# A spectral filter and token MLP with its backward pass on one core: half of the column tables by symmetry, the first turned tile in quarters, four row moves issued by GpSimd, eleven fillers moved forward

## The chip, the core and the metric

The kernel runs on one core of a Trainium2 chip. The core has TensorE (PE; its weight loads are listed as PEld), VectorE (DVE), ScalarE (ACT), GpSimd (POOL) and SyncE (SP), which run their own instruction streams in order and wait for each other by semaphores; DMA transfers are issued by one of them and carried out by 16 DMA engines. The metric is device time in microseconds (us) of one execution; lower is better. The time before is the median of three runs, 345.46 us (343.97 to 347.54).

## The reference

Forward and gradient of two residual blocks on x of 2048 x 448 in bf16 (S = 2048 tokens, D = 448, F = 1792):

```
h  = x + irfft2( rfft2( layernorm(x) ) * (w_r + i w_i) )        # over both axes, 225 columns kept
h2 = h + ( gelu( layernorm(h)^T w1 + b1 ) w2 + b2 )^T            # the MLP mixes tokens
out, vjp = jax.vjp(f, x, w_r, w_i, w1, b1, w2, b2)
return out, *vjp(grad_out)
```

Eight outputs: h2 and the gradients of x, w_r, w_i, w1, b1, w2 and b2. The two-dimensional transform is done as matmuls with tables of sines and cosines.

## The kernel before

**Stages.** The forward transform has a *row part* and a *stage 2*. In the row part the 16 row tiles of x (128 rows of 448) are normalized, folded (left half plus and minus the mirrored right half, `fold_prep`; from the fifth pair on in quarters, `fold_quarters`), and go through two steps on TensorE: `row_a(t)` multiplies the fold by a 128 x 128 table scaled by the row's standard deviation (`scale_R`), and `row_b(h)` multiplies by the column tables `csF` (or `csQ`, the even columns of them, reordered by GpSimd at line 926). csF has sine and cosine (index w, cosine 0, sine 1), two blocks b, and KW = 226 columns, and is made by `gen_fwd_d`: VectorE computes the angles and reduces them, ScalarE takes the Sin. Each pair of row_b steps fills one tile `cs`, which a DMA moves into `D2` with its rows spread over 32 partitions (line 689, eight moves of 226 KB; the tiles lie in the buffers r452, rX). Stage 2 (`s2_stage`) is a transform over the other factor of the rows: for five steps s, 48 small matmuls out of D2, ScalarE copies, VectorE multiplies with the filter W, 48 small matmuls back, and moves into `D3` (line 727, sixteen of 113 KB, issued by GpSimd). Then `inv_rows` transforms D3 back, and the MLP and the backward pass follow, from 96 us on.

**Fillers.** Independent of all this is the first product of the backward MLP, grad_out times w2 transposed: 14 column tiles j of w2 with 16 matmuls of 448 columns each, 224 in all. `dg_gen` is a generator which gives one of them at each step, and `fill(n)` puts n of them into TensorE's stream at that place. FILL_A and FILL_B say how many stand ahead of and behind each row step t; more stand between the tables and in stage 2 (7 and 7 in each of its five steps), and `drain()` behind stage 2 puts out what is left, 37 of them behind the last 7 of stage 2. w2 must be transposed for it: tiles 0 to 3 come as they are and are turned on TensorE (`turn_w2`, 16 transposes of 128 x 128 in two groups of eight, each copied from PSUM by ScalarE at line 319), tiles 4 to 13 by a transposing DMA (line 312) into a ring of five buffers (three in rE, two in rO): tile j + 5 is loaded when tile j is used up, but no more than CAP tiles before the rows are done; the ones held back are loaded in front of the last 14 fillers ahead of stage 2.

**Order.** The streams of TensorE, VectorE, ScalarE and SP keep the order in which the program calls them; GpSimd's is set by a planner. A move into D2 is put off by RESH_LAG = 1.1 us of TensorE's planned time (`defer`) and then stands in SP's stream. So that stream has in one line the transposing DMAs, the 18 loads of W (line 591) and the D2 moves. `evac` gives a PSUM copy to ScalarE or VectorE by a running sum of estimated costs, so a change ahead of it can turn over who copies what.

Names that matter below: `D2` lies in r2 (matmuls from it are listed at line 225, `ps_ff<-r,Vt`), `D3` in r3 (`ps_ff<-RTm,r` at line 220 is its first use), fillers are `ps_mm<-rC,rE` or `rC,rO` at line 220, row_a is `ps_ff<-rX,rS`, row_b `ps_ff<-csF,rS` or `ps_ff<-r,rS`. VectorE's and ScalarE's operations nearly all have line 84, a recording helper.

Of the kernel before, what the change touches and what calls it, by code (L numbers as in the profile page):

```python
# [12 lines left out]
I32 = mybir.dt.int32  # L13
# [8 lines left out]
KW = 226  # L22
# [4 lines left out]
KC = 113  # L27
# [10 lines left out]
CAP = 9  # L38
# [86 lines left out]
def kernel(  # L125
# [188 lines left out]
    def turn_w2(j, parts=(0, 8)):  # L314
        for h in parts:
            pt = (ps_mm if j < 2 else ps_ff)()[:].bitcast(BF16).rearrange("p (t c) -> p t c", c=P)
            for t in range(8):
                nc.tensor.transpose(pt[:, t, :], w2n[j][:, h + t, :], ident[:])
            sc.copy(out=w2Ts[j][:, h:h + 8, :], in_=pt)
# [54 lines left out]
    for _ in range(20):  # L374
# [6 lines left out]
             channel_multiplier=0, allow_small_or_imprecise_dtypes=True)  # L381
    krow = ftmp(0, D)
# [49 lines left out]

    def gen_fwd_d(late):
        t = ftmp(576, 2, KW)
        t2 = ftmp(1028, 2, KW)
        q = ftmp(1536, 2, KW)
        q2 = ftmp(2048, 2, KW)
        js = []
        for o in (1.0, 225.0):
            js.append(col())  # L440
            ve.tensor_scalar(out=js[-1], in0=pcol, scalar1=2.0 / 896.0, scalar2=o / 896.0, op0=ALU.mult, op1=ALU.add)
        chains = []
        s_ = Later(sc, late)
        for w, u, v, ph in ((1, t, q, 0.0), (0, t2, q2, 0.25)):
            chain = []
            v_ = Later(ve, chain)
            for b in range(2):
                v_.tensor_scalar(out=u[:, b, :], in0=krow[:, 0:KW], scalar1=js[b], scalar2=ph, op0=ALU.mult, op1=ALU.add)
            v_.tensor_scalar(out=v, in0=u, scalar1=MAGIC, scalar2=MAGIC, op0=ALU.add, op1=ALU.subtract)
            v_.tensor_tensor(out=v, in0=u, in1=v, op=ALU.subtract)  # L450
            s_.activation(out=csF[:, w, :, :], in_=v, func=ACT.Sin, scale=s1)
            chains.append(chain)
        for pair in zip(*chains):
            for fn in pair:
                fn()
        s_.copy(out=csF[:, 0, :, 0:1], in_=rAT[:, 0:2].rearrange("p (b o) -> p b o", o=1))
# [209 lines left out]
    def row_b(h, quarters=None):  # L666
# [21 lines left out]
        if c:  # L688
            defer(RESH_LAG, lambda: resh[0].dma_start(out=D2[u:u + 125:4, 8 * e:8 * e + 8].rearrange("p g c k -> p (g c k)"),
                                                      in_=cs.rearrange("p x c k -> p (x c k)")), cs)  # L690
# [133 lines left out]
    def dg_gen():  # L824
        pgs = {}
        turns = {(0, 3): 1, (1, 11): 2, (2, 4): 3}
        order = [(j, 4 * q + i) for q in range(4) for j in range(2) for i in range(4)]
        for j, t in order + [(j, t) for j in range(2, NFB) for t in range(NT)]:
            if not t:
                pgs[j] = ps_mm()  # L830
            mm(pgs[j][:, 0:D], lhsT=w2Ts[j][:, t, :], rhs=go_tp[:, t, :], start=(t == 0), stop=(t == NT - 1))
            if (j, t) in turns:
                turn_w2(turns[j, t])
            if t == NT - 1:
                evac(out=dgu[:, j, :], in_=pgs.pop(j)[:, 0:D])
                if w2T_ring.i >= cap[0]:
                    held_w2.append(load_w2T)
                else:
                    load_w2T()
            yield  # L840
# [10 lines left out]
    for fn in r_ops:  # L851
        fn()
    ve.tensor_scalar(out=ident[:], in0=krow[:, 0:P], scalar1=pcol, scalar2=None, op0=ALU.is_equal)
# [17 lines left out]
    turn_w2(0, (0,))  # L871
# [4 lines left out]
    turn_w2(0, (8,))  # L876
# [26 lines left out]
    FILL_B = (0, 0, 0, 2, 2, 2, 2, 2, 2, 2, 2, 2, 2, 2, 2, 2)  # L903
# [531 lines left out]
```

## Time and profile before

| | us |
|---|---|
| median of 3 runs | 345.46 (343.97 to 347.54) |
| profiled execution | 345.03 |
| its span (first to last instruction) | 343.3 |
| TensorE busy in the span | 329.5 |
| VectorE / ScalarE / GpSimd busy | 250.8 / 206.7 / 73.7 |

By stage, from the view of busy time in windows (us from the start of the span; DMA is the mean busy share of the 16 DMA engines, by packet times that can overlap):

| stage | window | TensorE busy | VectorE busy | ScalarE busy | DMA |
|---|---|---|---|---|---|
| loads, first rows | 0 to 16.2 | 12.8 | 14.4 | 12.1 | 0.91 |
| rows 4 to 9 | 16.2 to 31.7 | 14.1 | 15.1 | 11.4 | 1.00 |
| rows 10 to 15 | 31.7 to 43.5 | 11.8 | 7.1 | 8.3 | 1.03 |
| tables, until stage 2 | 43.5 to 50.3 | 4.6 | 3.0 | 3.1 | 1.04 |
| stage 2 | 50.3 to 70.8 | 20.2 | 15.0 | 14.9 | 1.12 |
| fillers behind it | 70.8 to 79.1 | 8.3 | 1.3 | 3.5 | 0.54 |
| inverse rows | 79.1 to 96.0 | 16.3 | 13.1 | 15.5 | 0.98 |
| MLP and backward pass | 96.0 to 343.3 | 241.3 | 181.8 | 137.9 | 0.88 |

The granted TensorE clock was 1.00 in every window. In a line of a stream the first two numbers are start and duration in us, then engine, line, operation, output and inputs, and how many are merged; in square brackets stands the idle time of the engine before it and what ended it. A line with SPq or POOLq is the issuing of a DMA, not its transfer.

### The profile page before, as it was taken

The page shows a single profiled execution, that of the slowest core. Times are in us where ns is not written, and L with a number is a line of the kernel's source. Part 1 is how long each engine was busy: PE and PEld are TensorE (multiplying, and loading weights), DVE is VectorE, ACT ScalarE, POOL GpSimd, SP SyncE. Part 2 cuts the span into 40 slices and gives each one's busy share as a digit, 9 for nine tenths or more (in the row PEclk, how much of TensorE's full clock was granted, in tenths as well). Part 3 has the DMA queues.
Part 4 walks back from the last instruction along what each step waited for, and adds up shares of the span by engine and source line. Part 5 has one row for each costly group of instructions (what it writes and reads, how often), then busy time and mean ns, then how long its engine had stood idle before and what let it go on. Part 6 is the DMA issues. An engine that isn't in the chain of part 4 may idle for free.

```text
span 343.3 us, 7935 instructions
## 1 busy us (share of the span) xinstructions
PE 329.5 (96%) x2868; PEld 173.6 (51%) x2877; DVE 250.8 (73%) x669; ACT 206.7 (60%) x447; POOL 73.7 (21%) x235
## 2 busy tenths in 40 slices
PE   8798979999999999999999999999999999999995
PEld 4475644456645555555555555554333334555552
DVE  8999438724966888594325988786589985599993
ACT  5987647856966553513221346565488875688882
POOL 7766202441220000001001111110000000156660
PEclk9999999999999999999999999999999999999999
DMA  7999999979899999767976988836898898999975
GB/s 265 397 171 179 173 262 174 185 144 253 242 346 307 333 278 253 177 204 221 207 179 137 169 190 180 169 96 186 223 288 236 214 262 244 295 238 295 231 289 203
DMA packets 138606, 78.03 MB, mean 227 GB/s; under 512 B 88072, under 2 KB 130440, under 8 KB 138440
## 3 DMA queue, kind: packets, MB, share of 16 engines
q1 hardware_dynamic: 137000, 75.28, 86.9%
q0 software_dynamic: 1280, 1.86, 3.0%
q8 instruction: 22, 0.36, 0.5%
q10 hardware_dynamic: 288, 0.39, 0.3%
q14 instruction: 16, 0.13, 0.1%
HBM read 27.81 MB, written 22.04 MB: 145 GB/s over the span
## 4 chain that ended last, share of the span: by engine, by line
PE 69%; DVE 2%; ACT 1%; issue 1%; POOL 0%; DVEq 0%; ACTq 0%
PE ps_mm L220 62%; PE ps_ff L220 6%; PE ps_ff L225 2%; DVE rA L84 1%; ACT rO L84 1%; DVE r L84 0%; ACT rC L84 0%; DVE rS L84 0%; DVE rO L84 0%; DVE rB L84 0%; POOL lcol L1183 0%; ACT rAT L84 0%; DVEq L1430 0%; ACT r L84 0%; ACT rstd_h L84 0%
## 5 line engine op out<-in xcount | busy, mean ns | idle before, releaser
L220 PEld LDWEIGHTS <-r 128*128 128x128 bf16 (+2 forms) x628 | 58.5, 105 | 47.3 <-issue 2.8
L220 PEld LDWEIGHTS <-rS 128*128 128x128 bf16 (+1 forms) x468 | 36.2, 97 | 34.9 <-issue 6.4
L84 ACT CAST rO<-ps_mm 128x512 bf16<-128x512 f32 (+1 forms) x70 | 37.3, 583 | 15.9 <-PE ps_mm L220 14.1
L220 PE MATMUL ps_mm<-rD,r 128*128 128x448 bf16 x224 | 44.5, 352 | 0.0
L220 PEld LDWEIGHTS <-rst 128*128 128x128 bf16 (+1 forms) x320 | 23.5, 97 | 31.4 <-issue 14.1
L220 PE MATMUL ps_mm<-rC,rE 128*128 128x448 bf16 x144 | 31.5, 353 | 0.9 <-ACT rE L84 0.9
L220 PE MATMUL ps_mm<-rB,r 128*128 128x448 bf16 x160 | 31.2, 352 | 0.1
L220 PE MATMUL ps_mm<-rG,rst 128*128 128x512 bf16 (+1 forms) x121 | 26.8, 380 | 1.1 <-issue 0.8
L220 PE MATMUL ps_mm<-r,rst 128*128 128x512 bf16 (+2 forms) x144 | 27.4, 345 | 0.0
L84 ACT CAST r<-ps_ff 128x452 bf16<-128x452 f32 x44 | 23.9, 586 | 5.2 <-PE ps_ff L225 3.0
L84 ACT ACTIVATE r<-ps_mm,rstd_h 128x448 bf16<-128x448 f32 x16 | 10.1, 634 | 26.8 <-PE ps_mm L220 26.8
L84 DVE SCALAR_TENSOR_TENSOR r<-ps_mm,b2col,r 128x448 bf16<-128x448 f32 x16 | 10.9, 682 | 19.9 <-PE ps_mm L220 18.2
L84 ACT ACTIVATE r<-rC 128x448 bf16<-128x448 bf16 x16 | 9.1, 571 | 26.7 <-DMA out_dram<-r 22.5
L1183 POOL TENSOR_SCALAR lcol<-lcol 128x1 f32<-128x1 f32 x16 | 8.5, 530 | 64.7 <-ACT r L84 64.7
L84 ACT ACTIVATE rG<-rG 128x896 bf16<-128x896 bf16 x14 | 13.3, 950 | 14.9 <-DVE rG L84 14.7
L220 PEld LDWEIGHTS <-rO 128*128 128x128 bf16 (+1 forms) x165 | 15.2, 98 | 12.0 <-ACT rO L84 0.2
L220 PE MATMUL ps_ff<-csI,rAT 113*128 113x224 bf16 (+1 forms) x108 | 19.0, 298 | 0.6 <-ACT rAT L84 0.4
L84 ACT CAST rS<-ps_ff 128x512 bf16<-128x512 f32 x31 | 18.0, 584 | 2.0 <-PE ps_ff L220 1.7
L1356 POOL TENSOR_SCALAR lcol<-lcol 128x1 f32<-128x1 f32 x16 | 3.7, 234 | 70.7 <-ACT r L84 69.6
L220 PE MATMUL ps_mm<-rC,rO 128*128 128x448 bf16 x80 | 18.5, 353 | 0.0
L220 PEld LDWEIGHTS <-rE 128*128 128x128 bf16 x144 | 13.0, 98 | 10.6 <-ACT rE L84 1.2
L84 DVE TENSOR_SCALAR rG<-rG 128x896 bf16<-128x896 bf16 x28 | 10.9, 389 | 10.0 <-ACT rG L84 10.0
(197 smaller groups left out, 639.6 us busy)
## 6 DMA issues: line engine op xcount, KB each, us to landing
out_dram<-rO SPq DMA_DIRECT2D x34, 256.0 KB
r<-in_B_w_dram SPq DMA_DIRECT2D x5, 1024.0 KB
r<-r SPq DMA_DIRECT2D x12, 226.0 KB
r<-in_B_w_dram SPq DMA_DIRECT2D x3, 896.0 KB
rS<-in_B_w_dram SPq DMA_DIRECT2D x3, 896.0 KB
out_dram<-rG SPq DMA_DIRECT2D x10, 256.0 KB
rB<-in_B_w_dram SPq DMA_DIRECT2D x4, 512.0 KB
rO<-in_B_w_dram SPq DMA_DIRECT2D x2, 1024.0 KB
```

The source lines that it names most:

```text
L84: fn(**kw)
L220: nc.tensor.matmul(out, lhsT=lhsT, rhs=rhs, start=start, stop=stop)
L225: nc.tensor.matmul(out, lhsT=lhsT, rhs=rhs, start=start, stop=stop)
L1183: gp_.tensor_scalar(out=m1, in0=ms, scalar1=-1.0 / D, scalar2=None, op0=ALU.mult)
L1356: gp_.tensor_scalar(out=m1, in0=ms, scalar1=-2.0 / D, scalar2=None, op0=ALU.mult)
```

## The change

- `gen_fwd_d` computes 113 of the columns of each table (KC = 113) in one array instead of 226 in two, with one Sin for all; the other 112 are the mirrored columns of the other table (sine from cosine and the reverse), times +1 or -1 by the parity of the partition, in two VectorE copies. The column at the end is set to zero. The signs come from a GpSimd iota and two VectorE steps of one column.
- `turn_w2` takes groups of any size, and the first half of tile 0 is turned and copied in two groups of four. The first fillers are put in another order: tile 0 quarters 0 and 1, tile 1 quarters 0 and 1, then the others in turn.
- The four D2 moves with u >= 2 (the later half) are issued by GpSimd instead of SP.
- FILL_B gets 4 more fillers at row step 2, 3 at step 6, 2 each at steps 7 and 8; so `drain()` has 11 fewer. CAP is 10 instead of 9, which lets a tenth tile of w2 be loaded within the rows.

In the order of the instructions of the changed kernel, the load of that tenth tile stands in SP's stream between the third and the fourth D2 move, with loads of W around it, and the only GpSimd instruction between its four moves is a memset of csF's first column, which waits for the table's transposes (line 563 before). The two mirror copies stand in VectorE's stream behind the fold for rows 4 and 5. In the balance of copies, VectorE takes over three copies of row_a results and one of an inverse table, and gives up three row_b copies and one filler copy to ScalarE.

```diff
-CAP = 9
+CAP = 10
...
-    def turn_w2(j, parts=(0, 8)):
-        for h in parts:
+    def turn_w2(j, parts=((0, 8), (8, 8))):
+        for h, n in parts:
             pt = (ps_mm if j < 2 else ps_ff)()[:].bitcast(BF16).rearrange("p (t c) -> p t c", c=P)
-            for t in range(8):
+            for t in range(n):
                 nc.tensor.transpose(pt[:, t, :], w2n[j][:, h + t, :], ident[:])
-            sc.copy(out=w2Ts[j][:, h:h + 8, :], in_=pt)
+            sc.copy(out=w2Ts[j][:, h:h + n, :], in_=pt[:, 0:n, :])
...
+    podd = col().bitcast(I32)
+    gp_.iota(podd, pattern=[[0, 1]], base=0, channel_multiplier=1, allow_small_or_imprecise_dtypes=True)
+    gp_.memset(csF[:, :, :, KW - 1:KW], 0.0)
...
     def gen_fwd_d(late):
-        t = ftmp(576, 2, KW)
-        t2 = ftmp(1028, 2, KW)
-        q = ftmp(1536, 2, KW)
-        q2 = ftmp(2048, 2, KW)
+        u = ftmp(576, 2, 2, KC)
+        q = ftmp(1028, 2, 2, KC)
...
+        for w, ph in ((1, 0.0), (0, 0.25)):
             for b in range(2):
-                v_.tensor_scalar(out=u[:, b, :], in0=krow[:, 0:KW], scalar1=js[b], scalar2=ph, op0=ALU.mult, op1=ALU.add)
-            v_.tensor_scalar(out=v, in0=u, scalar1=MAGIC, scalar2=MAGIC, op0=ALU.add, op1=ALU.subtract)
-            v_.tensor_tensor(out=v, in0=u, in1=v, op=ALU.subtract)
-            s_.activation(out=csF[:, w, :, :], in_=v, func=ACT.Sin, scale=s1)
...
+                ve.tensor_scalar(out=u[:, w, b, :], in0=krow[:, 0:KC], scalar1=js[b], scalar2=ph, op0=ALU.mult, op1=ALU.add)
+        ve.tensor_scalar(out=q, in0=u, scalar1=MAGIC, scalar2=MAGIC, op0=ALU.add, op1=ALU.subtract)
+        ve.tensor_tensor(out=q, in0=u, in1=q, op=ALU.subtract)
+        Later(sc, late).activation(out=csF[:, :, :, 0:KC], in_=q, func=ACT.Sin, scale=s1)
+        v_ = Later(ve, late)
+        for w in range(2):
+            v_.tensor_scalar(out=csF[:, w, :, KC:2 * DC + 1], in0=csF[:, 1 - w, :, DC - 1::-1], scalar1=sgn, scalar2=None, op0=ALU.mult)
...
-            defer(RESH_LAG, lambda: resh[0].dma_start(out=D2[u:u + 125:4, 8 * e:8 * e + 8].rearrange("p g c k -> p (g c k)"),
+            defer(RESH_LAG, lambda: (gp_ if u >= 2 and quarters is csQ else nc.sync).dma_start(out=D2[u:u + 125:4, 8 * e:8 * e + 8].rearrange("p g c k -> p (g c k)"),
...
-        order = [(j, 4 * q + i) for q in range(4) for j in range(2) for i in range(4)]
+        order = [(j, 4 * q + i) for j, q in ((0, 0), (0, 1), (1, 0), (1, 1), (0, 2), (1, 2), (0, 3), (1, 3)) for i in range(4)]
...
+    ve.tensor_scalar(out=podd, in0=podd, scalar1=1, scalar2=None, op0=ALU.bitwise_and)
+    ve.tensor_scalar(out=sgn, in0=podd, scalar1=-2.0, scalar2=1.0, op0=ALU.mult, op1=ALU.add)
...
-    turn_w2(0, (0,))
+    turn_w2(0, ((0, 4), (4, 4)))
...
-    turn_w2(0, (8,))
+    turn_w2(0, ((8, 8),))
...
-    FILL_B = (0, 0, 0, 2, 2, 2, 2, 2, 2, 2, 2, 2, 2, 2, 2, 2)
+    FILL_B = (0, 0, 4, 2, 2, 2, 5, 4, 4, 2, 2, 2, 2, 2, 2, 2)
```

More of the change, by code (lines that the diff above doesn't have):

```diff
@@ L430, in gp_madd @@
         gp_.tensor_tensor(out=out, in0=gtmp, in1=in1, op=ALU.add)
+    sgn = col()
     def gen_fwd_d(late):
-        t = ftmp(576, 2, KW)
-        t2 = ftmp(1028, 2, KW)
-        q = ftmp(1536, 2, KW)
-        q2 = ftmp(2048, 2, KW)
+        u = ftmp(576, 2, 2, KC)
+        q = ftmp(1028, 2, 2, KC)
         js = []
@@ L441, in gen_fwd_d @@
             ve.tensor_scalar(out=js[-1], in0=pcol, scalar1=2.0 / 896.0, scalar2=o / 896.0, op0=ALU.mult, op1=ALU.add)
[L442 to L446, printed above, removed]
-            for b in range(2):
-                v_.tensor_scalar(out=u[:, b, :], in0=krow[:, 0:KW], scalar1=js[b], scalar2=ph, op0=ALU.mult, op1=ALU.add)
-            v_.tensor_scalar(out=v, in0=u, scalar1=MAGIC, scalar2=MAGIC, op0=ALU.add, op1=ALU.subtract)
-            v_.tensor_tensor(out=v, in0=u, in1=v, op=ALU.subtract)
-            s_.activation(out=csF[:, w, :, :], in_=v, func=ACT.Sin, scale=s1)
[L452 to L456, printed above, removed]
+        for w, ph in ((1, 0.0), (0, 0.25)):
+            for b in range(2):
+                ve.tensor_scalar(out=u[:, w, b, :], in0=krow[:, 0:KC], scalar1=js[b], scalar2=ph, op0=ALU.mult, op1=ALU.add)
[5 more added lines that the diff above has]
+            v_.tensor_scalar(out=csF[:, w, :, KC:2 * DC + 1], in0=csF[:, 1 - w, :, DC - 1::-1], scalar1=sgn, scalar2=None, op0=ALU.mult)
+        Later(sc, late).copy(out=csF[:, 0, :, 0:1], in_=rAT[:, 0:2].rearrange("p (b o) -> p b o", o=1))
     def gen_R(ve, sc):
```

## The prediction

> **What bounds the kernel now.** I read the page's busy row first, then who TensorE waited for, then the streams of TensorE, SP and POOL one by one in order of time.
>
> ```profile
> PE 329.5 (96%) x2868; PEld 173.6 (51%) x2877; DVE 250.8 (73%) x669; ACT 206.7 (60%) x447; POOL 73.7 (21%) x235
> ```
>
> TensorE is busy for 329.5 of 343.3 us, so all idle time is 13.8 us, and the change neither adds nor removes a matmul of the fillers. It can only win idle time back. The waits of TensorE in the first 110 us (what, line, for whom: us in total, times, longest) say where that is:
>
> ```profile
> PE ps_ff L225 <- DMA r<-rX: 2.2, 1, 2.2
> PE ps_ff L220 <- ACT csF L84: 1.3, 1, 1.3
> ...
> PE ps_ff L220 <- DVE rS L84: 1.0, 2, 0.7
> PE ps_mm L220 <- ACT rE L84: 0.9, 2, 0.5
> ...
> PE ps_ff L220 <- DVE rX L84: 0.3, 1, 0.3
> ```
>
> 3.5 us lie in the row steps (1.3 + 1.0 + 0.9 + 0.3), all before 31.7 us; after that the rows run without a gap. Then comes 2.2 us before stage 2, for the last moves into D2. TensorE's stream in order of time (start, us) shows both ends of stage 2:
>
> ```profile
> 45.31 2.81 PE L220 MATMUL ps_mm<-rC,rE 128*128 128x448 bf16 x14
> 50.34 0.63 PE L225 MATMUL ps_ff<-r,Vt 32*32 32x452 bf16 x16 [2.22 <-DMA r<-rX]
> ...
> 70.79 5.47 PE L220 MATMUL ps_mm<-rC,rE 128*128 128x448 bf16 x28
> 76.09 3.19 PE L220 MATMUL ps_mm<-rC,rO 128*128 128x448 bf16 x16
> 79.12 0.83 PE L220 MATMUL ps_ff<-RTm,r 128*113 128x128 bf16 x12
> ```
>
> The rows end at 43.5; fillers last until 48.1; D2 is complete at 50.3. Behind stage 2, 44 fillers (28 + 16) cover the moves into D3 until 79.1. SP's stream shows why D2 is late, and when D3 has landed:
>
> ```profile
> 38.43 3.84 SPq L312 DMA_TRANSPOSE rO<-in_B_w_dram  x1
> 42.37 0.59 SPq L689 DMA_DIRECT2D r<-r  x1
> 43.01 1.91 SPq L591 DMA_DIRECT2D rW<-in_A_w_i_dram  x3
> 45.02 0.58 SPq L689 DMA_DIRECT2D r<-r  x1
> 45.65 0.60 SPq L591 DMA_DIRECT2D rW<-in_A_w_i_dram  x1
> 46.36 2.57 SPq L689 DMA_DIRECT2D r<-rX  x4
> 49.02 2.02 SPq L312 DMA_TRANSPOSE rO<-in_B_w_dram  x1
> ...
> 77.34 0.42 SPq L1016 DMA_DIRECT2D r<-in_B_w_dram  x1
> ```
>
> SP issues without a pause from 13.5 to 49.0; the four late moves wait in that line (their data were evacuated by 44.4), and the last, issued at 48.4, is there 1.9 us later. The load at 77.34 waits for all D3 moves, so D3 is complete at about 77.3: the cover behind stage 2 is 79.1 - 77.3 = 1.8 us longer than needed. For POOL's moves there is a row of its own (below: its stream, and the landing times of its 16 moves of 113 KB):
>
> ```profile
> 71.67 2.36 POOL L727 DMA_DIRECT2D r<-r  x4 [1.27 <-ACT r L84]
> ...
> DMA to landing us min/median/max: 3.7/5.8/7.5
> ```
>
> **Column tables.** VectorE's stream has four 128x226 steps (1.08 us from start to end), two of 128x452 (0.69) and two subtractions (1.16): 2.68 us from 7.91 to 10.59. After it are four of 128x113 (0.8, between 0.6 by the 128x1 row of 144 ns and 1.1 by the 128x226 row), one of 128x452 (0.35) and one subtraction (0.58): 1.7, so 0.95 saved (0.65 to 1.15). Added are two 128x1 steps ahead of ident (0.15 each; VectorE waited 0.26 for x there, so 0.1 counts) and, behind the second pair's fold, two mirror copies of 128x224 (0.25 each, between the 128x128 bf16 step's 0.22 and the 128x512 one's 0.31). These wait for ScalarE's Sin, now one of 452 where two took 1.03; it ends at about 15.5, VectorE comes at 15.6, so the wait is nothing (0 to 0.5). Queued behind the mirrors are the statistics and row scales of all later rows. Net: the fold for row 4 comes 0.85 earlier, everything behind it 0.35 earlier (0.9 earlier to 0.3 later). POOL's added iota and memset (0.14 and 0.1 by the rows beside them) lie ahead of krow, which VectorE uses a microsecond later: nothing.
>
> **First turned tile in quarters, and the new order of the first fillers.** ScalarE's copy of 1024 columns took 1.01 us and held TensorE 0.43; two of 512 cost some 0.55 each, and four fillers then need only the first half. The second wait of 0.45 goes too, since fillers 5 to 8 now use the other quarter of tile 0. I take 0.8 off (0.4 if the second quarter of grad_out is late).
>
> **Eleven fillers.** One costs 0.195 us (16 in 3.19, 28 in 5.47), so 2.15 us move from the cover behind stage 2 into rows that had 3.5 us idle. Four fill the gap before row 4, three that before row 8, two each those before rows 9 and 10. VectorE's chain sets those rows, so the rows end where they did: 43.4 (42.2 if every gap closes; 45.7 if none does and the fillers simply add).
>
> **D2, which decides.** SP loses four issues (2.57 us), but they were the last ones. With the cap at 10, a fifth transpose is issued between the last two moves that stay on SP. The one that was issued at 45.02 now stands behind it. A transpose took SP 2.0 to 3.8 us in this stretch, so that move goes out at 47.1 to 48.9, and lands 1.9 (the row before) to 3 us later: 49.0 to 51.9, middle 50.4. On POOL the last late move goes out when its evacuation ends, 44.4, plus one issue of 0.59 ahead of it: 45.0. Landing takes 3.7 to 7.5 for half the bytes, plus 0.4 for the other half (0.3 at the 386 GB/s that the moves reached at 49 us, 0.75 at the 150 GB/s of 71 to 76): 49.0 to 53.3, 51.2 at the median row; if POOL were as quick as SP with the same move (1.9), 46.9; the memset between the last two waits for the table's transposes at 43.7, which are past. D2 needs both, so I take the later middle, 51.2 against 50.3: **stage 2 starts 0.9 us later**, with 3 us idle before it. The DMA engines were 1.06 busy from 44.0 to 50.3. The Trainium skill's entry page, "Trainium Kernel Development and Optimization", Key Constraints, says that the queues of SP and GpSimd share the same 16 engines and that issuing from several saves only issue time; by it the move to POOL is worth at most SP's 2.57 us of issuing. POOL's rows show 3.7 to 7.5 us to landing for 113 KB; "DMA: Bandwidth & Descriptors" (Anatomy of one DMA) fits 2.0 us plus bytes/436e3 for a GpSimd DMA, which makes 2.5 us for 226 KB, an estimate that the rows contradict. By the page POOL's moves would be in by 47.5 and SP alone would decide.
>
> **Behind stage 2.** The cover shrinks by 2.15, of which 1.8 was spare; TensorE then waits 0.35 for D3. The first copy of the next stage, held up by a filler's evacuation (0.44 wait at 80.40), gains 0.2. The rest of the kernel, from 96 us on, is TensorE's and unchanged. The transposes that were behind the late moves come earlier, so no filler waits.
>
> **Sum**, against the profiled execution's 345.03 us (span 343.3): -1.8 (fillers off the tail) -0.2 (the copy) +0.9 (D2) = -1.1, giving 343.9. What VectorE and the quarters save is not added: it becomes wait for D2. The median of the runs, 345.46, is 0.43 above the profiled one, so the prediction is **344.4**.
>
> **Rivals.**
> 1. *D2 comes early.* If the moved issues free both queues, with the transpose at 2.0 us and POOL at its shortest rows, D2 is complete at 49.0, or 1.3 earlier than before: -2.0 - 1.3 = -3.3, 342.2. At best TensorE sets the start: rows end at 42.2 with all gaps closed, 4.6 of fillers and table transposes behind them make 46.8, and -5.5, 340.0. For it: POOL's last four moves in the trace, with no other traffic, took 4.2. Against: here a transpose is under way.
> 2. *POOL's moves land late (slower).* Place: the last move, with a transpose on the same engines. At 7.5 us plus 0.8 and the 45.0 issue it is 53.3; with the two moves ahead of it still under way another 1.2 (two times the 0.59 issue pace): 54.5. Stage 2 starts 4.2 later, -2.0 + 4.2 = +2.2: 347.7. It decides from D2 at 52.3 on, where the gain of 2.0 is used up.
> 3. *The rows don't take the fillers.* If the folds are no earlier and the fillers fall beside the gaps, rows end at 45.7, POOL issues 2.2 later, D2 is complete at 53.4 and the gain is gone: -2.0 + 3.1 = +1.1, 346.6.
>
> **How the numbers follow.** Forecast (D2 between 50.2 and 52.2) 0.50, 343.4 to 345.4; rival 1 0.25; rival 2 0.15; rival 3 0.10. The range 341.8 to 346.9 leaves out the better half of rival 1 and the worse half of rival 2. 1% (3.45 us) is about what a measurement of this kernel can tell from no change. Faster than 342.0 needs D2 below 48.8, the better half of rival 1, with POOL near SP's 1.9: 0.15. Slower than 348.9 needs D2 beyond 55.8, the end of rival 2: 0.08. The rest, 0.77, lies between.
>
> **What would show it.** In the profile after: waits of TensorE on csF, rS, rX and rE down from 3.5 to about 1 us; the wait before stage 2 at 2 to 4 us, released by a move from POOL or the last one on SP; that one issued near 48 behind a transpose; POOL's moves with landings of 4 to 8 us; a short new wait of the RTm matmuls for D3. The prediction is wrong if the wait before stage 2 is under 1 us, or if POOL's landings pass 9 us.

## The result: 1.1% slower, and the profile after

The changed kernel takes 349.74 us (median of 4 runs, 347.72 to 352.09) where the kernel before takes 345.19 (4 runs): a ratio of 1.0112, 95% interval [1.0063, 1.0160]. The forecast was 344.4, the range ended at 346.9. The profiled execution took 348.66 us with a span of 346.8, against 345.03 and 343.3. Ratios and intervals leave out executions that lie over 1.5% above the fastest of their kernel (7 of 12 for the fillers alone, 4 of 12 for three parts with SP and cap 9, 3 of 10 for the gate, at most 2 elsewhere), so a ratio is not the quotient of the two medians.

The page of the changed kernel, the busy row and the row of the granted TensorE clock (40 slices of 8.7 us, in tenths):

```profile
PE 330.8 (95%) x2868; PEld 174.3 (50%) x2877; DVE 250.3 (72%) x671; ACT 206.2 (59%) x447; POOL 77.0 (22%) x241
PEclk9999998999999999999999999999999999999999
```

TensorE has the same 2868 matmuls, is busy 1.3 us longer, and idle for 16.0 us instead of 13.8. The one 8 in the clock row is the seventh slice, 52 to 61 us: the start of stage 2. Who TensorE waited for (what, line, for whom: us in total, times, longest):

```profile
PE ps_ff L225 <- issue: 4.9, 1, 4.9
PE ps_ff L220 <- DVE rS L84: 1.6, 2, 0.9
...
PE ps_mm L220 <- DMA rC<-in_grad_out_dram: 1.0, 1, 1.0
...
PE ps_ff L220 <- DMA r<-r: 0.6, 1, 0.6
```

In the rows the waits of 3.5 us have become two of 0.9 and 1.0 and one of 0.3 (forecast: about 1 in all). The wait in front of stage 2 has grown from 2.2 to 4.9. TensorE's stream (start, us) shows both, and a third thing:

```profile
43.04 0.99 PE L220 MATMUL ps_ff<-r,rS 112*128 112x113 bf16 x16
...
45.83 2.81 PE L220 MATMUL ps_mm<-rC,rE 128*128 128x448 bf16 x14
53.52 0.81 PE L225 MATMUL ps_ff<-r,Vt 32*32 32x452 bf16 x16 [4.88 <-issue]
...
54.67 4.04 PE L220 MATMUL ps_mm<-rC,rO 128*128 128x448 bf16 x14
...
75.37 3.39 PE L220 MATMUL ps_mm<-rC,rE 128*128 128x448 bf16 x17
78.59 3.19 PE L220 MATMUL ps_mm<-rC,rO 128*128 128x448 bf16 x16
81.62 0.83 PE L220 MATMUL ps_ff<-RTm,r 128*113 128x128 bf16 x12
```

Fourteen fillers took 2.81 us at 45.83 and 4.04 at 54.67. The view of windows gives the reason (window, length, PE busy and instructions, granted clock, DMA busy share, GB/s):

```profile
52.00:54.00 2.00, 0.48 (x36) 0.94 0.88 279
54.00:56.00 2.00, 2.00 (x44) 0.50 1.14 221
56.00:58.00 2.00, 2.00 (x9) 0.71 1.07 237
58.00:60.00 2.00, 2.00 (x56) 1.00 1.18 165
```

Behind the wait the clock ran at 0.50 for 3.41 us, from 53.75 (the trace's records of the clock). From the first matmul of stage 2 to the last group of fillers in it (53.52 to 75.37; 50.34 to 70.79 before) passed 21.85 us instead of 20.45.

SP's stream, and the landing times of the four moves that GpSimd now issues (at 39.72, 43.28, 44.68 and 45.26):

```profile
42.81 3.46 SPq L312 DMA_TRANSPOSE rO<-in_B_w_dram  x1
46.31 1.24 SPq L589 DMA_DIRECT2D rW<-in_A_w_i_dram  x2
47.65 0.58 SPq L687 DMA_DIRECT2D r<-r  x1
48.28 0.60 SPq L589 DMA_DIRECT2D rW<-in_A_w_i_dram  x1
48.98 11.76 SPq L312 DMA_TRANSPOSE rE<-in_B_w_dram  x3
```

```profile
DMA to landing us min/median/max: 5.6/9.0/9.3
```

The transpose of the tenth tile holds SP for 3.46 us; the fourth move of SP goes out at 47.65. The third move of GpSimd takes 8.7 us: 44.68 + 8.7 = 53.4, and stage 2 starts at 53.52.

Only the third of the four late moves decides that start. Each late move fills one half of D2's 16 groups (groups 0 to 7 or 8 to 15) on a quarter of its partitions, the first step of stage 2 reads groups 0, 2, 4 and 6, and the third move is the last that fills those. The trace's records of landings (a semaphore counts to 16 for each move) agree: in the changed kernel the third landed at 53.43, the fourth at 54.56 and the fourth move of SP at 56.14, both behind the start; in the kernel before the third landed at 50.21, stage 2 started at 50.34 and the fourth landed at 51.10. In the profiles of all the kernels below in which TensorE waited in front of stage 2, it started 0.09 to 0.14 us behind the third landing and ahead of the fourth.

**The account.** Rows end 0.5 later; the wait in front of stage 2 is 2.7 longer; stage 2 takes 1.4 longer at the low clock; eleven fillers less behind it take 2.1 off. That makes +2.5, and the inverse rows do start at 81.62 instead of 79.12. This stays until about 290 us. Another 0.9 comes late in the backward pass (a 0.6 wait for a move between 290 and 300 among it); it was not traced to the change. The other three executions had a mean granted clock of 0.983 to 0.990 where the profiled one had 0.995; two of them took longer (350.82 and 352.09 us), the one at 0.987 did not (347.72).

### The profile page after: what moved, and what is told of

Its sections match the earlier page's. It is cut to its first block, busy times and chain, and to the rows that moved or that the text cites. A ratio compares the mean times of both kernels' runs of the same rounds, so it can differ in the third digit from the quotient of the medians.

```text
span 346.8 us, 7946 instructions
## 1 busy us (share of the span) xinstructions
PE 330.8 (95%) x2868; PEld 174.3 (50%) x2877; DVE 250.3 (72%) x671; ACT 206.2 (59%) x447; POOL 77.0 (22%) x241
## 4 chain that ended last, share of the span: by engine, by line
PE 80%; ACT 6%; DMA 4%; DVE 3%; issue 3%; SPq 2%; POOL 0%; DVEq 0%; ACTq 0%
PE ps_mm L220 68%; PE ps_ff L220 8%; PE ps_ff L225 4%; DMA rA<-in_A_x_dram 2%; ACT rO L84 2%; ACT rX L84 1%; DMA r<-r 1%; DVE r L84 1%; SPq L329 1%; ACT r L84 1%; SPq L310 1%; DVE rA L84 1%; DVE stats L84 0%; DVE rS L84 0%; ACT rG L84 0%
## 5 line engine op out<-in xcount | busy, mean ns | idle before, releaser
L220 PEld LDWEIGHTS <-r 128*128 128x128 bf16 (+2 forms) x628 | 58.5, 105 | 48.1 <-issue 2.5
L84 ACT CAST rX<-ps_ff 128x452 bf16<-128x452 f32 x22 | 11.3, 584 | 11.7 <-PE ps_ff L225 9.6
L84 ACT CAST rG<-ps_mm 128x512 bf16<-128x512 f32 (+1 forms) x28 | 13.9, 542 | 6.8 <-PE ps_mm L220 6.7
```

The lines of the kernel that those rows point to most:

```text
L84: fn(**kw)
L220: nc.tensor.matmul(out, lhsT=lhsT, rhs=rhs, start=start, stop=stop)
```

## The experiments

Sixteen runs of fifteen kernels, each compared with the kernel before on the same chip. The table has fourteen of them (those with unread matmuls and with a gate stand in the text alone). It puts the profiled execution of each beside its ratio: the wait in front of stage 2, the start of stage 2, the start of the inverse rows, and, as a mean over all its executions, the time that the clock took, (1 - granted clock) x time. "Three parts" are tables, quarters with the new order, and the eleven fillers.

| kernel | ratio to before [95%] | wait | stage 2 | inverse rows | clock's share |
|---|---|---|---|---|---|
| before | 1 | 2.2 | 50.3 | 79.1 | 0.7 |
| changed (three parts, GpSimd, cap 10) | 1.0112 [1.0063, 1.0160] | 4.9 | 53.5 | 81.6 | 3.9 |
| three parts, SP, cap 10 | 1.0036 [1.0004, 1.0067] | 4.0 | 51.9 | 80.2 | 3.1 |
| three parts, GpSimd, cap 9 | 0.9985 [0.9954, 1.0016] | 1.5 | 49.8 | 77.2 | 1.0 |
| three parts, SP, cap 9 | 0.9992 [0.9958, 1.0026] | 2.2 | 50.4 | 78.0 | 2.1 |
| before, cap 10 | 1.0127 [1.0086, 1.0168] | 4.7 | 53.7 | 84.1 | 3.2 |
| before, GpSimd | 0.9955 [0.9926, 0.9984] | 1.4 | 49.4 | 78.1 | 0.8 |
| the same again | 1.0009 [0.9978, 1.0040] | 0 | 48.1 | 80.7 | 1.3 |
| before, GpSimd, 19 fillers ahead of stage 2 | 0.9998 [0.9957, 1.0039] | 0.3 | 49.3 | 77.7 | 0.9 |
| before, 23 fillers ahead | 0.9963 [0.9925, 1.0001] | 0.4 | 50.9 | 81.0 | 0.6 |
| before, 7 fillers ahead | 1.0044 [1.0007, 1.0081] | 3.3 | 49.9 | 81.6 | 2.5 |
| before, fillers of the change | 0.9968 [0.9924, 1.0011] | 3.2 | 51.2 | 82.7 | 2.7 |
| before, tables of the change | 1.0030 [1.0000, 1.0060] | 1.9 | 49.6 | 78.3 | 1.0 |
| before, cap 8 | 0.9989 [0.9955, 1.0023] | 0 | 48.9 | 78.3 | 0.7 |
| before, cap 8, tables, fillers | 0.9997 [0.9962, 1.0033] | 0.2 | 48.6 | 81.7 | 2.8 |
| three parts, SP, cap 8 | 0.9999 [0.9969, 1.0029] | 0 | 48.1 | 79.6 | 2.1 |

(The row of before has the profile shown ahead of the prediction, and the clock's share of 29 runs beside the last experiments; beside the others it was 1.0 to 1.1.)

### Moves back on SP; moves on GpSimd alone

The first theory was that GpSimd's landings make the loss. One run undoes them in the changed kernel, one puts them alone into the kernel before.

```diff
 # changed kernel
-    (gp_ if u >= 2 and quarters is csQ else nc.sync).dma_start(out=D2[...
+    resh[0].dma_start(out=D2[...
```

> The changed kernel with its four late row moves issued by SP again, all else as changed. If GpSimd's slow landings (9 us in the trace of the changed kernel, D2 complete at 53.5) are what delays stage 2, D2 is now set by SP's line: last W load issued until 48.9, four moves of 0.6 us behind it, the last landing 1.9 us after its issue, so D2 is complete at 52.5 to 53, the wait before stage 2 is 3.5 to 4.3 us and the time 347 to 349. If SP's line with the tenth tile in it were harmless and only GpSimd cost time, the wait would be back at the 2.2 us of the kernel before and the time at 344 to 345. If GpSimd's moves are not the cause, the time stays at 349.7.

347.97 us (10 runs), ratio 1.0036. Of the loss two thirds are gone, but not the wait:

```profile
PE ps_ff L225 <- DMA r<-rX: 4.0, 1, 4.0
```

All five last moves of SP now stand behind the tenth transpose (42.90 to 45.4), the four late ones go out from 48.12, and the clock falls to 0.50 from 52.4 to 55.8 as well.

> The kernel before with one edit: the four late row moves issued by GpSimd. SP's line then comes to the held-back transposes at 46.4 instead of 49.0. Theory: a move by GpSimd next to transposes lands 9 us after its issue; the last is issued at 45.0, D2 is complete at 53 to 54, TensorE waits about 5 us, its clock drops behind that, and the time rises by 4 to 5 us to 349 to 350. Rival: the tenth tile in SP's line is what costs, and GpSimd's moves alone land in 4 to 6 us: D2 at 49 to 51, time 344 to 346.

345.22 us (10 runs), ratio 0.9955: no loss, a gain. GpSimd's moves land in 4.1 to 6.1 us, the wait is 1.4 and the clock stays at 1.00. So GpSimd's moves by themselves cost no time. That they gain was put to a second trial, with a variant in which five more fillers fill the rest of the wait:

> The kernel before with the four late moves on POOL and nothing else, a second time, beside the others on one chip. Theory: the gain of the first time holds, ratio 0.993 to 0.998, a wait before stage 2 of 1 to 2 us, POOL's landings 4 to 6 us, a clock of 0.998 to 1.0 in three of four runs. Rival 'the first gain was chance': ratio 0.999 to 1.002.

> The kernel before with the four moves on POOL and five fillers more ahead of stage 2 (19 instead of 14), five fewer behind it. Theory: the wait of 1.4 us before stage 2 becomes 0.4, stage 2 starts where it did (49.4), D3 is complete at 77.2 and the inverse rows start then instead of at 78.05; the clock stays at 0.998 to 1.0 in nearly all runs: 343.5 to 345 median, ratio 0.990 to 0.995, 0.2 to 0.3% under the run beside it with the moves alone. Rival 'a turned tile or D3 is late instead': a wait of 1 us or more inside or behind stage 2, and no gain over the run beside it.

```diff
 # kernel before, moves on GpSimd
-    fill(14)
+    fill(19)
```

346.43 us, ratio 1.0009, and 344.59 us, ratio 0.9998 (12 runs each). The gain was not found again. The second profile shows why an early D2 need not pay. GpSimd's moves landed in 3.4 to 4.7 us and stage 2 began at 48.06 without a wait, but then TensorE waited inside it:

```profile
PE ps_ff L225 <- DVE rS L84: 3.0, 2, 1.6
```

VectorE's first product with W came at 53.11, though ScalarE's copies for it were done at 50.6, and the inverse rows started at 80.70, later than before. The wait had moved from D2 to the next operand: the last load of W, issued at 47.31, landed at 52.84, and behind the two waits (1.3 and 1.6) the clock fell as well, from 57.80.

### Only the cap

```diff
-CAP = 10
+CAP = 9
```

> The changed kernel with the cap on the transposes of the rows back at 9, so that the tenth transpose stands behind all moves and W loads in SP's line, as before; all the rest of the change stays. Theory 'the tenth transpose costs, the rest is a gain': SP's last move goes out at about 45, POOL's landings fall from 9.0 to about 5 us, stage 2 starts at 49 to 50 instead of 53.5, the clock stays at 1.00 there, VectorE's first product with W comes right behind the copy, and the time is 342 to 344 us, ratio 0.985 to 0.995, below the kernel with the POOL moves alone (0.9955). Rival 'rows filled with the eleven fillers, or the tables, cost something by themselves': the wait before stage 2 is 3 us or more although the tenth transpose is gone, and the time is within 0.3% of the kernel before or above it.

345.15 us (12 runs), ratio 0.9985. With all other parts in place, the loss is gone. Stage 2 in TensorE's stream, and the landings of GpSimd's first three moves (of the fourth, issued at 44.91, the trace has only a part, up to 51.15):

```profile
49.78 0.78 PE L225 MATMUL ps_ff<-r,Vt 32*32 32x452 bf16 x16 [1.49 <-ACT rD L84]
...
77.17 0.83 PE L220 MATMUL ps_ff<-RTm,r 128*113 128x128 bf16 x12
```

```profile
DMA to landing us min/median/max: 5.0/5.3/5.4
```

The third move, issued at 44.33, lands at 44.33 + 5.4 = 49.7, against 53.4 in the changed kernel, where it was issued 0.35 later and took 3.3 longer. The expected gain of 0.5 to 1.5% was not there either: the profiled execution is 1.4 us faster than that of the kernel before, the median 0.7, and the interval holds 1. By its ratio the run lies where the rival, a cost of the fillers or the tables, had put it; by its wait of 1.5 it does not.

The opposite trial puts the cap alone into the kernel before:

```diff
-CAP = 9
+CAP = 10
```

> The kernel before with cap 10 alone: one transpose more within the rows, in front of the late moves and the last W loads in SP's line; tables, copies, fillers and the moves on SP as before. Theory 'the tenth transpose in SP's line is the loss': SP's last late move goes out 2 to 4 us later than 48.4, the wait before stage 2 is 3.5 to 5 us instead of 2.2, the clock falls in most runs (0.995 or less), and the time is 347.5 to 350, ratio 1.004 to 1.012. Rival 'the transpose costs only together with POOL's moves': the wait stays at 2.2 to 3 us and the ratio is 0.998 to 1.003.

349.96 us (6 runs), ratio 1.0127: the whole loss, without any other part. It is also what the cap costs between the two kernels that differ by it alone, 1.0112 / 0.9985 = 1.0127 (with the two errors added in squares, 1.007 to 1.019). Its SP stream:

```profile
46.39 0.60 SPq L591 DMA_DIRECT2D rW<-in_A_w_i_dram  x1
47.08 2.05 SPq L312 DMA_TRANSPOSE rO<-in_B_w_dram  x1
49.25 2.55 SPq L689 DMA_DIRECT2D r<-rX  x4
51.89 8.68 SPq L312 DMA_TRANSPOSE rE<-in_B_w_dram  x3
```

The moves that went out from 46.36 in the kernel before go out from 49.25: 2.05 for the transpose in front of them, and 0.8 for rows that ended later in this execution. And TensorE:

```profile
53.65 0.81 PE L225 MATMUL ps_ff<-r,Vt 32*32 32x452 bf16 x16 [4.71 <-DMA r<-rX]
...
54.80 3.77 PE L220 MATMUL ps_mm<-rC,rE 128*128 128x448 bf16 x11
```

```profile
50.00:52.00 2.00, 0.00 (x0) 0.77 1.19 316
52.00:54.00 2.00, 0.35 (x17) 0.50 1.02 330
54.00:56.00 2.00, 2.00 (x52) 0.50 1.09 193
56.00:58.00 2.00, 2.00 (x7) 0.52 1.16 104
```

Here it is SP's moves for which TensorE waits, with no GpSimd in it; the clock falls within the wait, and eleven fillers take 3.77 us instead of 2.25. The inverse rows start 5.0 later than before.

The last corner of the square of caps and queues:

> The changed kernel with cap 9 and the moves back on SP: tables, quarters and the eleven fillers alone. With the changed kernel, the one with the moves on SP and the one with cap 9 it makes a square of two caps by two queues. Theory 'the two faults meet': at cap 9 POOL's moves are a small gain (this run 0.2 to 0.5% above the one with cap 9 and POOL, ratio 1.000 to 1.004), at cap 10 a loss; SP's last move goes out at about 48 and the wait before stage 2 is 2.5 to 3.3 us, with a lowered clock in half of the runs. Rival 'the queue of the moves does not matter at cap 9': ratio 0.997 to 0.9995, as with POOL.

346.42 us (12 runs), ratio 0.9992, wait 2.2. At cap 9 the queue of the moves makes no difference clear of noise (0.9992 and 0.9985; a clock of 0.995 or less in 7 of 12 and in 4 of 12 executions); at cap 10 it does: 1.0036 on SP, 1.0112 on GpSimd. So the loss of the changed kernel has two parts: a transpose in front of the moves, which costs either queue, and landings beside GpSimd's moves, the one that decides going from 5.4 to 8.7 us when that transpose is issued before it and not behind. It is not GpSimd's landings alone that are late there: in the changed kernel the tenth transpose took 11.6 us to land and SP's fourth move 8.5, with the moves on SP 4.7 and 3.1. The size of the first part is open: on SP cap 10 cost 1.27% in the kernel before and some 0.4% with the three parts (1.0036 to 0.9992). There the transpose was issued 4.2 us earlier (42.90 instead of 47.08) and the late moves 1.1 earlier, which fits, but no run separates it.

### What the clock costs

```diff
 # kernel before: seven of the fillers ahead of stage 2 are left for the tail
-    fill(14)
+    fill(7)
```

> The kernel before with seven of the fourteen fillers ahead of stage 2 left for the tail behind it: nothing else changes, no move and no load, but TensorE waits 1.4 us longer for D2 (3.6 instead of 2.2), and the tail is 1.4 longer. Theory 'a wait at stage 2 of over 3 us lets the clock fall, and that is a good part of what the changed kernel lost': time 1.4 longer by the tail and 1.5 to 1.7 by the clock in most of the runs, which show 0.990 to 0.995: 348 to 349.5, ratio 1.007 to 1.012. Rival 'the clock does not follow from this wait': the runs show the clocks of the kernel before, ratio 1.003 to 1.005.

348.89 us (12 runs) against 345.92 beside it, ratio 1.0044. The edit changes nothing ahead of stage 2 but the time for which TensorE waits. Its stream:

```profile
49.94 0.65 PE L225 MATMUL ps_ff<-r,Vt 32*32 32x452 bf16 x16 [3.30 <-DMA r<-rX]
50.83 4.51 PE L220 MATMUL ps_mm<-rC,rE 128*128 128x448 bf16 x14
```

Fourteen fillers took 4.51 us, 1.7 more than the 2.81 at full clock. Ten of the 12 executions had a mean clock of 0.995 or less; of the 35 of the kernel before beside them 16 had. The median is 3.0 higher, which is the 1.4 of seven fillers and 1.6 more; the ratio makes it 1.5 in all, which lies in the range of the rival, so the time alone does not tell the two apart. The clocks and the profile do, for the theory: in this profile a wait of 3.3 us is charged about one and a half times, once as a wait, and by 1.7 again through the clock.

The reverse, unread matmuls (26 of them, added work) in the wait of the changed kernel:

```diff
     fill(14)
+    warm_ps = ps_mm()
+    for _ in range(26):
+        nc.tensor.matmul(warm_ps[:, 0:D], lhsT=Rm[:], rhs=go_tp[:, 0, :], start=True, stop=True)
```

> The changed kernel with 26 matmuls of 448 columns added in front of stage 2, whose result nobody reads; they fill some 5 us of the wait. Theory: the granted clock fell to 0.61 to 0.69 for 5 us because TensorE had stood idle for 4.9 us, and that cost 1.5 us (stage 2 took 21.85 us instead of 20.45); with TensorE busy the clock stays at 1.00, stage 2 still starts at about 53.5, and the time falls by 1.0 to 1.5 us to 348.2 to 348.7. Rival: the clock falls whatever TensorE does, or the matmuls push stage 2 back: 349.7 or more.

The clock stayed at 1.00 at the start of stage 2 and 14 fillers took 2.82 us, as the theory says; but the time was 352.16 us (4 runs), ratio 1.0152 [1.0085, 1.0218], and the rival held. In this execution the third late move landed at 50.16, 3.3 us earlier than in the changed kernel's, and the unread matmuls kept stage 2 from starting until 53.29. And the wait had moved:

```profile
PE ps_ff L225 <- DVE rS L84: 4.0, 2, 2.4
```

VectorE's first product with W came at 59.38 only; in this execution the tenth transpose held SP for 5.29 us, and the last load of W, behind it, went out at 51.48 and landed at 59.0. The clock then fell from 61.6 to 68.4 us. The tenth transpose delays the filter as it does the moves.

Nine fillers more ahead of stage 2 in the kernel before, in place of its wait:

```diff
-    fill(14)
+    fill(23)
```

> The kernel before with nine fillers more ahead of stage 2 (23 instead of 14) and so nine fewer behind it: TensorE does 1.76 us of matmuls where it waited 2.2 for D2. Theory: stage 2 starts where it did (50.3), the inverse rows 1.7 earlier (77.4, when D3 is complete), no wait long enough for the clock to fall: 342.5 to 344, ratio 0.992 to 0.997, clock 0.998 to 1.0 in nearly all runs. Rival 'D2 comes later when TensorE is busy, or the fillers want a turned tile that is late': a wait of over 1 us stays and the ratio is 0.998 or more.

346.38 us (12 runs), ratio 0.9963 with an interval that just holds 1; eight of the 12 had a clock of 0.998 or more. The wait in front of stage 2 was down to 0.4, and a new one of 1.5 stood inside it, which the profile puts to nothing it knows:

```profile
69.27 4.49 PE L220 MATMUL ps_mm<-rC,rE 128*128 128x448 bf16 x14 [1.51 <-issue]
```

### Room in SP's line: hold the transposes back

Gate: in the changed kernel the transposes behind the rows wait for stage 2's first copy, by a small transfer of its result into an unread tile.

```diff
-    cap[0] = NFB
-    while held_w2:
-        held_w2.pop(0)()
     fill(14)
+    def release():
+        nc.sync.dma_start(out=gate[:], in_=Xs[:, 0, 0, 0:8])
+        cap[0] = NFB
+        while held_w2:
+            held_w2.pop(0)()
...
-    s2_stage(lambda s: set_of(Xs, s), fwd_mult, 7, 7, 0, split=True)
+    s2_stage(lambda s: set_of(Xs, s), fwd_mult, 7, 7, 0, {0: release}, split=True)
```

> The changed kernel with the four transposes behind the rows held back until stage 2 has copied its first result (a small transfer on SP that reads this result stands in front of them). Theory: GpSimd's landings are long because a transpose is under way on the same engines; without it the last two land 4 to 6 us after issue, D2 is complete at 49.5 to 51.5, the wait is 1 to 3 us, and the time is 345 to 347. Rival: 9 us is what 226 KB cost on GpSimd's queue by itself, or the tenth tile is what holds it: D2 stays at 53 to 54, time 349 to 350.

349.03 us (10 runs), ratio 1.0055 [1.0017, 1.0093]. The loss is half of that of the changed kernel, but the two intervals overlap, so it is not shown that holding back the later transposes saves anything; the tenth is still in the rows. Its profiled execution, 3 us above its median, began stage 2 at 49.80 and waited afterwards: 6.2 us for VectorE's products (the last load of W landed at 60.06) and 1.8 for a transposed tile.

One transpose fewer in the rows:

```diff
-CAP = 9
+CAP = 8
```

> The kernel before with one transpose fewer within the rows (cap 8 instead of 9), nothing else. Theory 'a transpose in SP's line costs the late moves its own 3 to 4 us': the late moves go out some 2 to 3 us earlier (issued from 43 to 46 as their data come, the last at about 45.5), D2 is complete at 47.5 to 48.5, stage 2 starts up to 2 us earlier, and the time is 343.5 to 345, ratio 0.991 to 0.997; the transposes that come later then feed later fillers, whose wait shows if they are late (0 to 1 us). Rival 'the transposes cost nothing, the rows' evacuations set the last move': stage 2 starts at 49.5 or later, ratio 0.998 to 1.003. Rival 'the transposes are wanted early': fillers wait for turned tiles behind stage 2 and the ratio is above 1.003.

345.20 us (12 runs), ratio 0.9989. D2 was complete before TensorE came (48.90, no wait), but rows ended 0.7 later and 0.6 were lost to a transposed tile; nothing is gained. With the fillers of the change taken in as well, twice:

> The kernel before with cap 8, the symmetric tables and the eleven fillers in the rows (moves on SP, copies in halves). Theory 'a late D2 is the loss: without transposes in SP's line the fillers are a gain': D2 is complete when TensorE comes to stage 2 (wait under 0.5 us), stage 2 starts at 47.5 to 49, D3 is complete 27 us later as in the kernel before (50.34 to 77.34), the inverse rows start at 75.5 to 76.5 instead of 79.1, the clock is 0.998 to 1.0 in most runs, and the time is 342 to 343.5, ratio 0.988 to 0.995. Rival 'D3 or the second half's turned tiles set the end whatever stage 2 does': TensorE waits behind stage 2 for D3 or for a turned tile, and the ratio is 0.996 or more.

> The changed kernel with cap 8 and the four moves back on SP: tables, quarters and eleven fillers stay. Theory as for the run beside it, and the quarters and the new order of the first fillers are worth 0 to 0.8 us more: ratio 0.986 to 0.995, inverse rows at 75 to 76.5. Rival 'the new order wants grad_out's second quarter too early': a wait for it of 0.7 to 1.0 us as in the changed kernel, and a time equal to or above that of the run beside it.

346.64 and 347.04 us (12 runs each), ratios 0.9997 and 0.9999. D2 was in time, as the theory had it, and still nothing was won; the rival held:

```profile
48.56 0.63 PE L225 MATMUL ps_ff<-r,Vt 32*32 32x452 bf16 x16 [0.19 <-DMA r<-rX]
...
53.43 5.04 PE L220 MATMUL ps_mm<-rC,rO 128*128 128x448 bf16 x13 [3.94 <-DMA rO<-in_B_w_dram]
```

(cap 8 with tables and fillers on the kernel before.) The eleven fillers in the rows use up turned tiles 2.1 us earlier, and the next one has not landed: 3.9 us, and 13 fillers at the low clock in 5.04 us instead of 2.6. With cap 9 the same fillers waited for no turned tile in front of the inverse rows (three parts with either queue, the fillers alone), so of the caps tried it is 9 that suits them, and the 10 of the change was not needed.

### Fillers alone, tables alone

```diff
-    FILL_B = (0, 0, 0, 2, 2, 2, 2, 2, 2, 2, 2, 2, 2, 2, 2, 2)
+    FILL_B = (0, 0, 4, 2, 2, 2, 5, 4, 4, 2, 2, 2, 2, 2, 2, 2)
```

> The kernel before with the eleven fillers moved into the rows alone (tables, copies, moves and cap as before). Theory 'the fillers do not fit into the row gaps without the quicker tables': rows end 0.5 to 1.5 us later, the wait before stage 2 stays at 1 to 2.2 us, the tail behind stage 2 is 2.1 shorter, so the time is 344.5 to 346, ratio 0.995 to 1.000. Rival 'they fill the gaps': rows end where they did, and the time falls by 1.8 to 2.1 us, ratio 0.994 to 0.995. Rival 'they add in full': rows end 2 us later, all evacuations and moves too, ratio 1.000 to 1.003.

Two kinds of executions: four with a clock of 0.998 to 1.0 and 343.09 to 344.85 us, eight with 0.983 to 0.990 and 347.95 to 352.52. The ratio 0.9968 counts the four and the quickest of the eight; the median of all, 348.77, is 2.9 above that beside it. The profiled execution is one of the eight: a wait of 3.16 in front of stage 2, then a clock of 0.50. The fillers did fit into the rows (they end at 43.5, as before); D2 was 0.9 later in this execution, and the wait passed 3 us.

The tables (diff as in the change):

> The kernel before with the column tables by symmetry alone. Theory: the fold for row 4 comes 0.8 earlier and its wait of 1.3 us for the table shrinks to about 0.5, but SP's last moves still set stage 2's start, at 49.5 to 50.3, so the time is that of the kernel before within 0.2%: 345.0 to 346.5, ratio 0.997 to 1.001. Rival 'the mirrors wait for the Sin and hold VectorE's later folds': waits for rS and rX in rows 5 to 10 grow by more than 1 us and the ratio is above 1.002.

346.42 us (12 runs), ratio 1.0030 with an interval that begins at 1. The wait of 1.3 for csF in front of row 4 is down to 0.6 for a fold, and the one of 0.7 in front of row 8 is up to 1.2. Nothing is won by them alone.

## Why the prediction was wrong, step by step

- **Column tables: right in size.** The chain took 7.92 to 9.77 us instead of 7.91 to 10.59: 0.83 saved, 0.95 forecast. The fold for row 4 came only 0.28 earlier (15.32), not 0.85, because VectorE then waited 0.43 for x. Row 4 has no wait in the changed kernel all the same.
- **Quarters: below the lower end.** Both waits for the copies went (0.9), and the case named for the range came true, but larger, a wait of 1.0 for the second quarter of grad_out. Nothing is left of the 0.8, nor of the 0.4 named for that case.
- **Eleven fillers: right.** The rows end at 44.0 instead of 43.5, within the range of 42.2 to 45.7, and the tail behind stage 2 is 2.1 shorter.
- **"D2, which decides": the step that failed.** The term is GpSimd's landing: 5.8 us, the median row of the moves into D3, plus 0.4 for the second half of the bytes, from 45.0 on, which made 51.2. The move that decided measured 8.7 (the second 9.2, the fourth 9.3), and stage 2 started at 53.52, 3.2 later than before instead of 0.9 and 0.2 beyond the end of the interval. Two choices made the term too small: the median row, and 150 to 386 GB/s for the second half. At the 82 to 103 GB/s that the engines moved here, 113 KB are 1.1 to 1.4 us, and with the longest row that makes 8.6 to 8.9; this was worked out after the fact. With cap 9 the same moves landed in 5.0 to 5.4 and stage 2 started at 49.8, better than the middle. The prediction counted the tenth transpose against the one move of SP behind it, not against the loads of W there, and against GpSimd's moves only in the rivals.
- **"D2 needs both": wrong, without harm to the sum.** What it calls D2 complete at 50.3 is the third landing; the last move, issued at 48.37, landed at 51.10, after 2.7 us and not 1.9. SP's fourth move was forecast for 47.1 to 48.9 and went out at 47.65, but it landed at 56.14 where 49.0 to 51.9 was forecast. The first step of stage 2 does not read it, so this second error did not show.
- **"With 3 us idle before it": the wait that had no price.** The forecast set a 3 us wait beside a start at 51.2 and charged it as time alone. A wait of 3.2 to 4.9 us took the clock to half in every profile that had one in front of stage 2: 0.9 to 1.7 us each in the fillers directly behind it. This term was missing, and without it the landing does not explain the miss: with the measured start, 3.2 later, the prediction's own sum gives 346.7, still inside its range; with the 1.4 us by which stage 2 was longer it gives 348.1, outside. The rest up to 349.7 is the 0.9 late in the backward pass and the profiled execution's being 1.1 below the median.
- **Behind stage 2: close.** The forecast 0.35 us wait for D3 did not come: SP's load that waits for all moves stands at 81.34, the inverse rows at 81.62, so the cover is used up to 0.3.
- **The rivals.** The second is the one that came true in its mechanism (a late landing of GpSimd's moves with a transpose on the same engines), at 15%. It put the last landing at 54.5, and it was 54.56; but stage 2 did not wait for it, and the 347.7 lacks the clock, so its nearness to the measured time is in part luck. The sign named for being wrong, landings beyond 9 us, was met (9.2 and 9.3). Where the rival says why, it has half: the cap by itself costs 1.27% without GpSimd. The first rival's condition (D2 early) was also met, in the experiments, and does not pay: TensorE then waits for W or for a turned tile.

So the likeliest case failed at one place in the kernel, one transposing DMA moved ahead of D2's moves, and by two terms: a landing taken too short and a clock that had no price. No variant beats the kernel before by more than can be measured; the one candidate with an interval below 1, the moves on GpSimd alone, was 0.9955 once and 1.0009 the second time.

## What to carry to other kernels

A DMA put earlier into an in-order issuing stream is charged to everything behind it, to what comes two operands later, and to moves of other queues that share the engines; take a landing time only from a row with the same traffic in front of it, and ask which of several moves the next step really reads. A wait of TensorE that grows to about 3 us or more (here already 1.5 behind a stage of small matmuls) is to be priced by a second term, the matmuls that run at half clock behind it. Where several operands arrive just in time through one saturated path, moving one earlier shows the next one as late; look for that one before counting the gain.

## What the runs showed of the hardware

- **The clock behind a wait.** Waits in front of stage 2 of 1.4 to 2.2 us left the clock at 1.00 in the profiles (before 2.2; three parts with SP and cap 9 2.25); with waits of 3.16, 3.30, 4.0, 4.7 and 4.9 us it went to 0.50, within the wait or behind it, for 3.41 us (with 4.7 for 6.83). The Trainium skill, "TensorE: Matmul & The Clock Gate", Part 1, gives an idle window of about 3.4 us, after which the array runs at half its clock; 3.16 and 3.30 lie just under that. Three profiles disagree with a rule on the length of one wait: in the run with 23 fillers the clock fell behind a wait of 1.51 us, in that with the fillers alone behind a second one of 1.86, in the second run of GpSimd's moves behind two of 1.34 and 1.63, all among the 32 x 32 matmuls of stage 2.
- **The clock changes on a grid.** The records of the clock in the traces settle a part of this. From 10 us on it fell twelve times in the 18 profiles, each time for 3.41 us or for 6.83, twice that, and each fall lies a whole number of steps of 3.413 us ahead of the fall at the end of its profile (in the changed kernel 53.75 and 347.30, 86.0 steps; with the fillers alone 50.74, 71.22 and 347.70, 6.0 and 81.0). So the place of a wait on this grid counts, and not its length alone: the 2.2 us of the kernel before lay across two steps (1.5 and 0.7 us), while with cap 10 alone 2.1 us in one step came before the fall. Counted by steps, the matmuls other than the 32 x 32 ones were, as recorded, busy for at most 1.27 us in each step that a fall followed. Of the nearly 1700 steps at full clock without a fall behind them two lie below that (1.24 and 1.25, with 0.86 and 0.68 of 32 x 32 matmuls), all others at 1.5 or more. This fits a count of work by steps in which 32 x 32 matmuls weigh less; no run varied it.
- **The mean clock counts the falls.** One fall of 3.41 us at half clock is 1.7 us, or 0.005 of the time, and the clocks of the executions lie near 1.0, 0.995, 0.990 and 0.985. One kernel differs from run to run by their number: the fillers alone gave 344 us at 1.0 and 348 to 352 at 0.990 and below.
- **GpSimd's landings depend on what is ahead of them:** 226 KB took 3.4 to 6.1 us with the tenth transpose issued behind them (one landing is missing, at least 6.2); with it ahead the last three took 8.7 to 9.3 in the changed kernel, and the longest 11.8 and 11.1 in the runs with unread matmuls and with the gate, where the third took 5.7 and 5.2. In those two the transpose was issued at 44.2, just ahead of the third move, in the changed kernel at 42.81, ahead of the second. So the size of this term varies from execution to execution. The same 226 KB on SP's queue took 2.3 to 4.1 us for the late moves in all runs. In the changed kernel the engines moved little while they were busy:

```profile
48.00:50.00 2.00, 0.64 (x4) 1.00 1.07 82
50.00:52.00 2.00, 0.00 (x0) 1.00 1.32 103
```

82 and 103 GB/s at a DMA busy share over 1; the same kernel with cap 9 moved 288 in 48 to 50, the kernel before 368, and the changed kernel with its moves on SP 270 and 329 in the same two windows. "DMA: Bandwidth & Descriptors" of the Trainium skill (Queues, rings and completion order) says that an engine takes packets in turn from the queues that have work; that fits, but no run here separates the queues' sharing from the order in which the moves were issued. It stays open.
- **A transposing DMA holds SP** for 1.9 to 7.5 us ahead of 62 us in these runs (a move 0.5 to 1.8), and that of the tenth tile for 2.05 us with the cap alone and 5.29 in the run with unread matmuls.
